# Attention with each head on one half of the array's rows, its scores and values sharing two PSUM banks, and v of each batch in its own buffers

## Chip, cores and metric

The kernel runs on one core of one Trainium2 chip. The metric is the device time of one execution in microseconds (us). Three runs of the kernel before gave 643.86, 646.71 and 646.88 us; the median, 646.71 us, is the time before.

## What is computed

The attention of 2 batches and 8 heads over 576 positions with 64 features per head, then two feed-forward layers on the 1152 tokens. Heads 0 to 3 see the last 32 positions, heads 4 to 7 see every fourth of the last 128 positions, so each query has 32 keys.

```
scores = scale * (q @ k.T)
rel = pos[:, None] - pos[None, :]
mask_plain = (rel >= 0) & (rel < 32)                      # heads 0..3
mask_dil = (rel >= 0) & (rel < 128) & (rel % 4 == 0)      # heads 4..7
attn = softmax(where(mask, scores, -1e9))
x = attn @ v                                              # [2, 8, 576, 64] -> [1152, 512]
h = x @ w_in;  x = (h * tanh(softplus(h))) @ w_out        # 512 -> 2048 -> 512
p = probs / (probs.sum(-1) + 1e-9)
out = sum_e p[:, e] * (relu(x @ w1[e]) @ w2[e])           # 4 experts, 512 -> 1024 -> 512
```

## The kernel before

**Units.** The attention is cut into 10 units: 2 batches by 5 chunks of 128 positions (the last chunk of a batch has 64). I number them 0 to 9. A unit holds all 8 heads of its chunk, as 4 pairs of heads; the two heads of a pair lie on partitions 0 to 63 and 64 to 127 of the transposed q and k. Pairs 0 and 1 are the plain heads, pairs 2 and 3 the dilated ones, whose positions are sorted by their remainder modulo 4, so that every block of 32 queries needs a run of 64 keys.

**One unit's work.** `load_qk` brings k and q in natural layout. `transposes` (L309) turns them on TensorE. `spread` (L318 to L324) copies them on ScalarE from PSUM to `kk` and `qq`. In `kk` the copy is spread: head 0 of a pair goes to columns j=0 on partitions 0 to 63, head 1 to columns j=1 on partitions 64 to 127, and the other halves are zero (`zero_k`, L210, on VectorE). A score matmul (L338, L343) has a block of 32 queries of both heads as its stationary operand (128 rows, 32 columns) and 128 columns of `kk` as its moving operand: 64 keys of one head and 64 of the other, with the zeros keeping the heads apart. The four query blocks write four strips of 32 partitions. Ahead of them `sel` and `msk` put the mask into the same PSUM bank (L330 to L333). `softmax` reads the maximum (L351) and subtracts it (L352) on VectorE and takes the exponential on ScalarE (L353); `sums` (L357 to L359) follows on VectorE. `probsT` (L365) transposes the probabilities, `probsT_copy` (L370, ScalarE) brings them to `pT`, `values` (L377, L381) multiplies 128-row blocks of `pT` by `vP` or `vD`, again with zeros beside each head's v (`zero_v`, L202 and L203, on GpSimd), `normalise` (L389, VectorE) divides, `xT` (L398) transposes back, and `x_hi` (L406, ScalarE) and `x_lo` (L410, VectorE) split x into a high and a low part for the layers.

**Banks.** Scores are in bank 2 (unit 1: bank 6), transposed probabilities in bank 3, values in bank 4, `xT` in bank 5, the transposes of k and q in banks 0 and 1 (unit 1: 4 and 5). Every bank is a tile of its own, 512 columns of float32.

**Order.** The order is written out by hand: each engine works through its instructions as the program issues them. `att_step(s)` issues, in this order: the copy of unit s-1's probabilities, the copies of v for unit s+1, `spread` of unit s+1, `scores` and `softmax` of unit s, `sums` and `values` of unit s-1, `xT` of unit s-2, `normalise` of s-1, `x_hi` and `x_lo` of s-2 (from s=5 on with a weight-decoding step between, `dec_dve` and `dec_act`), `transposes` of s+2, `probsT` of s, and then the loads. Unit 1's scores are issued in step 0 already. The last three units (`u3`, `u2`, `u1` are units 7, 8 and 9) are written out after the loop, mixed with the first matmuls of the first layer (`steps[0].first`, `steps[1].first` in two halves, `steps[0].second`).

**v.** v of a head pair lies in `vP` (plain) and `vD` (dilated): on partitions 32 to 63 (and 96 to 127) the block's own 32 keys, on 0 to 31 (and 64 to 95) the block before, which `copy_v` (L277, L279) copies on GpSimd. Both batches use the same buffer. `v_loads` says in which step which chunks are loaded; all loads go through the queue of SP in program order.

**Weights.** `dec_load` brings a packed half of w_in or w_out into one of four staging buffers (L132, L135), `dec_dve` (L151, L158) and `dec_act` (L168, L175, L176) unpack it. The first layer accumulates its output for the first 512 tokens in banks 0 to 3 (`steps[n].second`, L509) after L487.

Of the kernel before, what the change touches and what calls it, by code (L numbers as in the profile page):

```python
# [23 lines left out]
def kernel(  # L24
# [41 lines left out]

    def bank(n):
        return ps.tile([128, 512], F32, tag=f"bank{n}", name=nm("bank"))
# [130 lines left out]
    def zero_v(c):  # L199
        blk = slice(4 * c, min(4 * c + 4, S // 32))  # L200
        for j in range(2):
            POOL.memset(vP[64 * j:64 * j + 64, :, blk, 1 - j, :], 0.0)  # L202
            POOL.memset(vD[64 * j:64 * j + 64, :, 1 - j, c], 0.0)  # L203
            if c == 0:
                POOL.memset(vP[64 * j:64 * j + 32, :, 0, j, :], 0.0)
                POOL.memset(vD[64 * j:64 * j + 32, :, j, 0], 0.0)

    def zero_k(c):
        for j in range(2):
            DVE.memset(kk[64 * j:64 * j + 64, :, 1 - j, 128 * c + 128:128 * c + 256], 0.0)  # L210
# [7 lines left out]
    for lo in (0, 32):  # L218
        m = msk[lo:lo + 32, :]
# [6 lines left out]
    for j in range(2):  # L226
        DVE.memset(kk[:, :, j, 0:128], 0.0)
        DVE.memset(kk[:, 2:4, j, 128 * NCH:], 0.0)
    for j in range(2):
        DVE.memset(vD[64 * j + 32:64 * j + 64, :, j, NCH - 1], 0.0)  # L230
# [5 lines left out]
    zero_v(1)  # L236
    for g in range(4):
        for n in "ns" if g else "n":
            ACT.activation(sel[n][0:32, 32 * g:32 * g + 32], ident[0:32, 0:32], AF.Copy)
        for n in "f" if g else "sf":  # L240
            ACT.activation(sel[n][32:64, 32 * g:32 * g + 32], ident[32:64, 32:64], AF.Copy)

    t = bank(7)
# [3 lines left out]
    def msk_b(n):  # L247
        return msk.unsqueeze(1).to_broadcast([64, n, 64])

    def load_v(b, c0, c1):
# [3 lines left out]
        for j in range(2):  # L256
            own = slice(64 * j + 32, 64 * j + 64)
            for p in range(2):
                src = v[b, 2 * p + j:2 * p + j + 1]
                SP.dma_start(out=vP[own, p, g0:g1, j, :],  # L260
                             in_=bass.AP(src.tensor, src.offset + 32 * g0 * D, [[D, 32], [32 * D, g1 - g0], [1, D]]))
            src = v[b, 4 + j:5 + j]
            for p in range(2 if cf > c0 else 0):
                SP.dma_start(out=vD[own, p, j, c0:cf, :],
                             in_=bass.AP(src.tensor, src.offset + (2 * p * S + 128 * c0) * D,
                                         [[4 * D, 32], [128 * D, cf - c0], [1, 4 * D]]))
            if cf < c1:
                n = (S - 128 * cf) // 4
                SP.dma_start(out=vD[64 * j + 32:64 * j + 32 + n, :, j, cf, :],
                             in_=bass.AP(src.tensor, src.offset + 128 * cf * D, [[4 * D, n], [2 * S * D, 2], [1, 4 * D]]))  # L270

    def copy_v(c):

        g0, g1 = max(4 * c, 1), min(4 * c + 4, S // 32)
        for j in range(2):
            before, own = slice(64 * j, 64 * j + 32), slice(64 * j + 32, 64 * j + 64)
            POOL.tensor_copy(vP[before, :, g0:g1, j, :], vP[own, :, g0 - 1:g1 - 1, j, :])  # L277
            if c:
                POOL.tensor_copy(vD[before, :, j, c, :], vD[own, :, j, c - 1, :])  # L279


    v_loads = {-2: (0, 2, NCH), 2: (1, 0, 2), 4: (1, 2, 4), 5: (1, 4, NCH)}

    class Unit:
        def __init__(self, b, c):
# [5 lines left out]
            self.tbanks, self.sbank, self.s = ((4, 5), 6, None) if second else ((0, 1), 2, None)  # L291
# [20 lines left out]
        def spread(self):  # L312
            n, t0 = self.n, 128 * self.c
            for j in range(2):
                rows = slice(64 * j, 64 * j + 64)
                o = slice(128 + t0, 256 + t0)
                if n == 128:
                    ACT.activation(kk[rows, :, j, o], self.pt[0][rows], AF.Copy)  # L318
                else:
                    ACT.activation(kk[rows, 0:2, j, 128 + t0:128 + t0 + n], self.pt[0][rows, 0:2, 0:n], AF.Copy)  # L320
                    dst, src = (x.rearrange("p a (r i) -> p a r i", r=4)[:, :, :, 0:n // 4]
                                for x in (kk[rows, 2:4, j, o], self.pt[0][rows, 2:4]))
                    ACT.activation(dst, src, AF.Copy)
            ACT.activation(qq[:, :, t0:t0 + n], self.pt[1][:, :, 0:n], AF.Copy)  # L324

        def scores(self):
            n, c = self.n, self.c
            self.s = s = bank(self.sbank)
            if self.first:
                PE.matmul(s[:, 0:256], sel["s"], msk_b(4), start=True, stop=False, skip_group_check=True)  # L330
                PE.matmul(s[:, 256:512], sel["f"], msk_b(4), start=False, stop=False, skip_group_check=True)
            else:
                PE.matmul(s, sel["n"], msk_b(8), start=True, stop=False, skip_group_check=True)  # L333
# [6 lines left out]
            kr = kk.rearrange("p a j (c r i) -> p a j c r i", r=4, i=32)  # L340
            for p in range(2):
                for r in range(4):
                    PE.matmul(s[32 * r:32 * r + n // 4, 256 + 128 * p:384 + 128 * p],  # L343
# [598 lines left out]
```

## Time and profile before

| | |
|---|---|
| runs, median (lowest to highest) | 646.71 us (643.86 to 646.88) |
| profiled execution | 646.41 us |
| its span in the profile | 644.6 us |
| TensorE busy, share of the span | 98% |
| VectorE, ScalarE, GpSimd busy | 46%, 41%, 27% |
| granted TensorE clock, mean | 0.997 of full speed |

The profiled execution's own time is 1.8 us longer than the span that the profile shows, and 0.3 us below the median of the three runs. Times within the profile are in microseconds from the start of the span. Matmuls are pipelined: a line of the timeline gives the first start of a group and the time to the end of its last one, so a group's length holds the time for which one matmul passes through the array; how fast matmuls follow each other is read from the starts.

### The profile page before, as it was taken

How to read it: one execution, taken by the hardware profiler on the slowest of the kernel's cores; microseconds unless marked ns; L12 is line 12 of the kernel's file. 1: busy time of each engine (PE TensorE's matmuls, PEld its weight loads, DVE VectorE, ACT ScalarE, POOL GpSimd, SP SyncE). 2: the span in 40 equal slices, each digit the busy share in tenths (PEclk: the TensorE clock that was granted, in tenths of full speed). 3: DMA queues.
4: the chain of work that ended last, by engine and by line, in shares of the span. 5: the costliest groups of instructions: out<-in, count | busy, mean ns of one | idle time of the engine just before them, and what ended most of it. 6: DMA issues, size and time to landing. Idle time of an engine off the chain costs nothing.

```text
span 644.6 us, 10166 instructions
## 1 busy us (share of the span) xinstructions
PE 630.8 (98%) x4154; PEld 562.7 (87%) x4154; DVE 299.0 (46%) x488; ACT 261.5 (41%) x497; POOL 177.0 (27%) x195
## 2 busy tenths in 40 slices
PE   8988999999999999999999999999999999999997
PEld 5766888889999999989998899898899998899986
DVE  7778777622211325464543622534623444624223
ACT  6667877633232344443344322344322443322220
POOL 6736555521200143270134300143300234200000
PEclk9989999999999999999999999999999999999999
DMA  9976576400000222210023200033100022000102
GB/s 182 193 161 174 195 224 221 142 1 1 1 1 1 65 66 66 66 67 2 0 75 92 94 2 1 1 99 98 67 1 0 31 76 91 1 2 15 51 1 81
DMA packets 51358, 43.66 MB, mean 68 GB/s; under 512 B 26352, under 2 KB 44144, under 8 KB 51312
## 3 DMA queue, kind: packets, MB, share of 16 engines
q1 hardware_dynamic: 51312, 43.02, 23.8%
q8 instruction: 32, 0.52, 0.3%
q14 instruction: 14, 0.11, 0.1%
HBM read 40.65 MB, written 2.36 MB: 67 GB/s over the span
## 4 chain that ended last, share of the span: by engine, by line
PE 93%; DMA 3%; DVE 1%; SPq 1%; issue 1%; ACT 1%; POOL 0%; DVEq 0%; ACTq 0%; POOLq 0%
PE bank L745 31%; PE bank L692 28%; PE bank L509 16%; PE bank L487 15%; DMA natq<-in_q_dram 2%; PE bank L309 1%; SPq L298 1%; DMA scr<-in_moe_w_out_dram 1%; PE bank L398 1%; PE bank L377 0%; PE bank L365 0%; DVE scr L158 0%; PE bank L381 0%; DMA vD<-in_v_dram 0%; PE bank L338 0%
## 5 line engine op out<-in xcount | busy, mean ns | idle before, releaser
L692 PE MATMUL bank<-xh,late 128*128 128x256 f32 (+1 forms) x512 | 120.6, 297 | 0.6 <-ACT late L704 0.5
L692 PE MATMUL bank<-wxh,late 128*128 128x320 f32 (+1 forms) x384 | 94.7, 296 | 0.0
L692 PEld LDWEIGHTS bank<-xh,late 128*128 128x128 f32 x512 | 88.3, 188 | 4.9 <-ACT late L704 2.0
L745 PE MATMUL bank<-late,gh 128*128 128x512 f32 x288 | 89.3, 391 | 0.0
L487 PE MATMUL bank<-xh,late 128*128 128x320 f32 (+1 forms) x288 | 76.5, 337 | 0.0
L692 PE MATMUL bank<-xl,late 128*128 128x256 f32 (+1 forms) x256 | 75.3, 294 | 0.0
L648 POOL TENSOR_TENSOR raw<-raw 128x256 f32<-128x256 f32 x16 | 12.2, 764 | 221.7 <-DVE late L537 217.7
L509 PE MATMUL bank<-gh,late 128*128 128x320 f32 (+1 forms) x288 | 72.6, 337 | 0.0
L692 PEld LDWEIGHTS bank<-wxh,late 128*128 128x128 f32 x384 | 67.8, 188 | 0.0
L496 DVE TENSOR_TENSOR gl<-scr,gh 128x512 fp32r<-128x512 f32 (+1 forms) x32 | 24.6, 769 | 84.5 <-ACT gh L495 84.5
L745 PEld LDWEIGHTS bank<-late,gh 128*128 128x128 f32 x288 | 52.3, 188 | 9.7
L710 DVE TENSOR_TENSOR raw<-bank,late 128x256 f32<-128x256 f32 (+1 forms) x32 | 14.6, 457 | 98.4 <-PE bank L692 91.2
L492 ACT ACTIVATE scr<-bank 128x320 f32<-128x320 f32 (+1 forms) x48 | 23.5, 490 | 85.7 <-PE bank L487 85.7
L537 POOL TENSOR_TENSOR late<-raw,late 128x1024 fp32r<-128x1024 f32 x16 | 38.6, 2413 | 66.4 <-ACT late L536 66.4
L745 PE MATMUL bank<-late,gl 128*128 128x512 f32 x144 | 56.7, 394 | 0.0
L692 PE MATMUL bank<-wxl,late 128*128 128x256 f32 (+1 forms) x192 | 56.3, 293 | 0.0
L536 ACT ACTIVATE late<-raw 128x512 fp32r<-128x512 f32 (+1 forms) x64 | 48.3, 783 | 18.3 <-PE bank L745 16.7
L487 PEld LDWEIGHTS bank<-xh,late 128*128 128x128 f32 x288 | 50.7, 188 | 4.3
L509 PEld LDWEIGHTS bank<-gh,late 128*128 128x128 f32 x288 | 50.1, 188 | 4.3
L745 PE MATMUL bank<-late,late 128*128 128x512 f32 (+1 forms) x219 | 52.8, 388 | 0.0
L692 PEld LDWEIGHTS bank<-xl,late 128*128 128x128 f32 x256 | 48.1, 188 | 2.5
L487 PE MATMUL bank<-xl,late 128*128 128x320 f32 (+1 forms) x144 | 48.6, 337 | 0.0
(146 smaller groups left out, 1175.0 us busy)
## 6 DMA issues: line engine op xcount, KB each, us to landing
raw<-in_moe_w_dram SPq DMA_DIRECT2D x32, 512.0 KB, 3.6
raw<-in_moe_w_in_dram SPq DMA_DIRECT2D x16, 512.0 KB, 4.4
raw<-in_moe_w_out_dram SPq DMA_DIRECT2D x8, 512.0 KB, 4.0
scr<-in_moe_w_out_dram SPq DMA_DIRECT2D x8, 512.0 KB, 3.8
natk<-in_k_dram SPq DMA_DIRECT2D x8, 256.0 KB, 4.7
natq<-in_q_dram SPq DMA_DIRECT2D x8, 256.0 KB, 5.1
out_dram<-scr SPq DMA_DIRECT2D x8, 256.0 KB, 2.0
vD<-in_v_dram SPq DMA_DIRECT2D x16, 64.0 KB, 3.6
```

The costliest lines, as they stand in the source:

```text
L298: SP.dma_start(out=t[0:self.n], in_=(k if x == "k" else q)[self.b, :, rows, :].rearrange("h t d -> t h d"))
L309: PE.transpose(o, nat[0:n, 128 * a:128 * a + 128], ident[0:n, 0:n])
L487: PE.matmul(h, a[:, c, :], x[:, c, :], start=c == 0 and k == 0, stop=c == 3 and k == 2)
L492: ACT.activation(self.hc[:, self.w * i:self.w * (i + 1)], h, AF.Mish)
L496: DVE.tensor_tensor(out=self.glo, in0=self.hc, in1=self.ghi.bitcast(F32), op=ALU.subtract)
L509: PE.matmul(yacc[self.grp][d], a[:, 512 + 128 * d:640 + 128 * d], x[:, g], start=u == UORD[self.grp][0] and k == 0, stop=u == UORD[self.gr ...
L536: ACT.activation(hi, src, AF.Copy)
L537: eng.tensor_tensor(out=lo, in0=src, in1=hi.bitcast(F32), op=ALU.subtract)
L648: POOL.tensor_tensor(out=a22, in0=a21, in1=a22, op=ALU.add)
L692: PE.matmul(out, w, x(k), start=first and k == 0 and i == 0, stop=k == 1 and i == 2, skip_group_check=not first)
L710: DVE.tensor_tensor(out=self.cb[:, 0:N], in0=self.c, in1=p1, op=ALU.add)
L745: PE.matmul(acc, x[:, s], a[:, cols], start=self.p == 0 and f == 0 and i == 0, stop=self.p == NP2 - 1 and f == 1 and i == 2, skip_group_ch ...
```

## The change

All eight banks become slices of one tile. `kk` loses its doubled layout and its zeros: one head of a pair is on partitions 0 to 63, the other on 64 to 127, and each matmul takes one head, 64 rows, as operands. Every score and value matmul is thus two, one on either half of the rows, with 64 moving columns in place of 128. The two halves write two banks: scores of head j go to bank 2+j, columns 0 to 255 (unit 1: banks 6 and 7), values of head j to bank 2+j, columns 256 to 511. Transposed probabilities move from bank 3 to bank 4, unit 1's transposes to banks 5 and 6. The mask is put in by two matmuls of 256 columns in place of one of 512. `spread` copies k in one instruction per unit (two for a chunk of 64) instead of two (four). `vP` and `vD` get a buffer for each batch and lose their zeros, and batch 1's v is loaded one step earlier. In the closing part `u1.normalise` is issued before `steps[0].second`.

```diff
+    banks = ps.tile([128, 4096], F32, name="banks")
     def bank(n):
-        return ps.tile([128, 512], F32, tag=f"bank{n}", name=nm("bank"))
+        return banks[:, 512 * n:512 * (n + 1)]
...
-    kk = ap1.tile([128, 4, 2, 128 * (NCH + 1)], F32, name="kk")
+    kk = ap1.tile([128, 4, 128 * (NCH + 1)], F32, name="kk")
-    vP = ap1.tile([128, 2, S // 32, 2, D], F32, name="vP")
-    vD = ap1.tile([128, 2, 2, NCH, 4 * D], F32, name="vD")
+    vP = [ap1.tile([128, 2, S // 32, D], F32, name=f"vP{b}") for b in range(B)]
+    vD = [ap1.tile([128, 2, NCH, 4 * D], F32, name=f"vD{b}") for b in range(B)]
-    msk = ap1.tile([64, 64], BF16, name="msk")
-    sel = {n: ap1.tile([64, 128], BF16, name=f"sel{n}") for n in "nsf"}
+    msk = ap1.tile([128, 64], BF16, name="msk")
+    sel = {n: ap1.tile([128, 128], BF16, name=f"sel{n}") for n in "nsf"}
+    HEAD = [slice(64 * j, 64 * j + 64) for j in range(2)]
...
-    for c in range(NCH):
-        zero_k(c)
-    zero_v(0)
+    for b in range(B):
+        for j in range(2):
+            DVE.memset(vD[b][64 * j + 32:64 * j + 64, :, NCH - 1], 0.0)
+            POOL.memset(vP[b][64 * j:64 * j + 32, :, 0, :], 0.0)
+            POOL.memset(vD[b][64 * j:64 * j + 32, :, 0], 0.0)
...
-    v_loads = {-2: (0, 2, NCH), 2: (1, 0, 2), 4: (1, 2, 4), 5: (1, 4, NCH)}
+    v_loads = {-2: (0, 2, NCH), 1: (1, 0, 2), 3: (1, 2, 4), 4: (1, 4, NCH)}
...
-            self.tbanks, self.sbank, self.s = ((4, 5), 6, None) if second else ((0, 1), 2, None)
+            self.tbanks, self.sbank, self.s = ((5, 6), 6, None) if second else ((0, 1), 2, None)
...
-            for j in range(2):
-                rows = slice(64 * j, 64 * j + 64)
-                if n == 128:
-                    ACT.activation(kk[rows, :, j, o], self.pt[0][rows], AF.Copy)
+            if n == 128:
+                ACT.activation(kk[:, :, o], self.pt[0], AF.Copy)
...
-            self.s = s = bank(self.sbank)
+            self.s = banks[:, 512 * self.sbank:512 * self.sbank + 1024].rearrange("p (j x) -> p j x", j=2)[:, :, 0:256]
+            s = [self.s[:, j] for j in range(2)]
...
-                    PE.matmul(s[32 * g:32 * g + 32, 128 * p:128 * p + 128], qq[:, p, t:t + 32],
-                              kk[:, p, :, t + 96:t + 160], start=False, stop=True, skip_group_check=True)
+                    for j, h in enumerate(HEAD):
+                        PE.matmul(s[j][32 * g:32 * g + 32, 64 * p:64 * p + 64], qq[h, p, t:t + 32],
+                                  kk[h, p, t + 96:t + 160], start=False, stop=True, skip_group_check=True)
...
         def probsT(self):
-            pt = bank(3).rearrange("p (s t) -> p s t", s=4)
+            pt = bank(4).rearrange("p (s t) -> p s t", s=4)
...
         def values(self):
-            self.x = x = bank(4).rearrange("p (s d) -> p s d", s=4)
+            self.x = banks[:, 1024:2048].rearrange("p (j x) -> p j x", j=2)[:, :, 256:512].rearrange(
+                "p j (s d) -> p j s d", d=D)
-                    PE.matmul(x[32 * g:32 * g + 32, p, :], self.pT[:, p, 32 * g:32 * g + 32],
-                              vP[:, p, 4 * c + g].rearrange("p j d -> p (j d)"), start=True, stop=True)
+                    for j, h in enumerate(HEAD):
+                        PE.matmul(self.x[32 * g:32 * g + 32, j, p], self.pT[h, p, 32 * g:32 * g + 32],
+                                  vP[b][h, p, 4 * c + g], start=True, stop=True, skip_group_check=True)
...
-        if 0 <= s < NCH - 2:
-            zero_v(s + 2)
...
     steps[0].split()
     dec_act()
+    u1.normalise()
     steps[0].second(lo_last=True)
-    u1.normalise()
```

## Rows read from the trace of the kernel before

**Rows 1.** The page's chain that ended last, shares of the span by engine.
```profile
PE 93%; DMA 3%; DVE 1%; SPq 1%; issue 1%; ACT 1%; POOL 0%; DVEq 0%; ACTq 0%; POOLq 0%
```

**Rows 2.** Busy time by stretch: stretch, length, each engine's busy us (instructions), granted clock, DMA.
```profile
100.00:110.00 10.00, 10.00 (x45) 8.05 (x44) 7.77 (x11) 7.39 (x13) 6.25 (x5) 1.00 0.67 213
```

**Rows 3.** TensorE timeline, unit 5's step: start, length, what, count, [idle before <-releaser].
```profile
30.58 0.28 PE L330 MATMUL bank<-msk,sels 64*128 64x256 bf16 x1
...
30.89 0.65 PE L338 MATMUL bank<-kk,qq 128*32 128x128 f32 x16
...
31.79 0.50 PE L377 MATMUL bank<-vP,pT 128*32 128x128 f32 x6
...
32.77 0.65 PE L398 MATMUL bank<-ident,xn 128*128 128x128 f32 x4
...
34.18 0.66 PE L365 MATMUL bank<-ident,pr 128*128 128x128 f32 x4
34.77 0.39 PE L333 MATMUL bank<-msk,seln 64*128 64x512 bf16 x1
```

**Rows 4.** VectorE timeline of the same step: maximum and subtraction of unit 5.
```profile
32.04 0.69 DVE L351 TENSOR_REDUCE mx<-bank 128x8 f32<-128x512 f32 x1 [0.35 <-PE bank L343]
32.77 0.69 DVE L352 TENSOR_TENSOR pr<-bank,mx 128x512 f32<-128x512 f32 x1
```

**Rows 5.** TensorE timeline: matmuls of 64 moving columns, and two on different strips.
```profile
20.57 0.41 PE L309 MATMUL bank<-ident,natq 64*128 64x64 f32 x4
...
27.05 0.28 PE L338 MATMUL bank<-kk,qq 128*32 128x128 f32 x2
```

**Rows 6.** Groups by line to 66 us: count, busy us, mean ns, idle before and releaser.
```profile
L210 DVE MEMSET kk<- 64x512 f32 x10 | 4.8, 485 | 1.5 <-issue 0.5
...
L318 ACT ACTIVATE kk<-bank 64x512 f32<-64x512 f32 x16 | 9.4, 587 | 1.3 <-PE bank L309 1.2
```

**Rows 7.** Chain that ended last, in order of time: two loads of q.
```profile
5.37 5.17 DMA natq<-in_q_dram
...
19.95 5.30 DMA natq<-in_q_dram
```

**Rows 8.** TensorE timeline: the values of units 5 and 6, with the idle time before.
```profile
37.58 0.64 PE L377 MATMUL bank<-vP,pT 128*32 128x128 f32 x16 [1.42 <-ACT pT L370]
...
43.67 1.02 PE L377 MATMUL bank<-vP,pT 128*32 128x128 f32 x16 [1.73 <-issue]
```

**Rows 9.** Busy time by stretch as in rows 2, around the values of unit 6.
```profile
40.36:43.77 3.41, 1.68 (x40) 1.04 (x42) 2.36 (x5) 1.94 (x4) 0.00 (x0) 1.00 1.15 218
43.77:47.18 3.41, 3.41 (x42) 2.70 (x42) 1.81 (x5) 2.54 (x5) 1.25 (x3) 0.50 0.57 99
```

**Rows 10.** Chain that ended last, in order of time, into the first layer.
```profile
50.25 3.89 DMA scr<-in_moe_w_out_dram
...
54.24 0.44 DVE scr L151
...
59.13 0.70 DVE pr L352
59.86 0.64 ACT pr L353
...
60.54 0.67 PE bank L365 x4
...
64.52 3.01 PE bank L509 x12
```

**Rows 11.** TensorE timeline: values of unit 8 and the transposes behind them.
```profile
56.94 0.64 PE L377 MATMUL bank<-vP,pT 128*32 128x128 f32 x16 [0.53 <-POOL vD L279]
...
57.95 0.66 PE L398 MATMUL bank<-ident,xn 128*128 128x128 f32 x4
```

**Rows 12.** VectorE timeline: normalise of unit 9, in two pieces.
```profile
65.11 0.74 DVE L389 TENSOR_TENSOR xn<-bank,sm 64x256 f32<-64x256 f32 x2
```

**Rows 13.** SP's queue: loads of batch 1's last chunk of v, then the weights.
```profile
45.74 2.59 SPq L260 DMA_DIRECT2D vP<-in_v_dram  x2
```

More of the change, by code (lines that the diff above doesn't have):

```diff
@@ L217 @@
     POOL.memset(msk, 0.0)
-    for lo in (0, 32):
-        m = msk[lo:lo + 32, :]
+    for o in range(0, 128, 32):
+        m, lo = msk[o:o + 32, :], o % 64
         POOL.affine_select(out=m, in_=m, compare_op=ALU.is_ge, fill=NEG, base=32,
@@ L225 @@
         DVE.memset(t, 0.0)
[L226 to L230, printed above, removed]
-    for c in range(NCH):
-        zero_k(c)
-    zero_v(0)
+    DVE.memset(kk[:, :, 0:128], 0.0)
+    DVE.memset(kk[:, 2:4, 128 * NCH:], 0.0)
+    for b in range(B):
[3 more added lines that the diff above has]
+            POOL.memset(vD[b][64 * j:64 * j + 32, :, 0], 0.0)
     for t in free_raws:
         POOL.memset(t[:, 4096:4104].bitcast(U32), 0)
[L236 to L241, printed above, removed]
+    for o in range(0, 128, 32):
+        eye = ident[o:o + 32, o:o + 32].unsqueeze(1)
+        for n, g0, g1 in (("n", 0, 4), ("s", 1, 4)) if o % 64 == 0 else (("f", 0, 4), ("s", 0, 1)):
+            dst = sel[n][o:o + 32, 32 * g0:32 * g1].rearrange("p (g i) -> p g i", i=32)
+            ACT.activation(dst, eye.to_broadcast([32, g1 - g0, 32]), AF.Copy)
     t = bank(7)
@@ L245, with msk_b @@
         PE.matmul(t, warm[:, 0:128], warm, start=n == 0, stop=n == NWARM - 1)
[L247 to L248 removed]
+    def msk_b(j, n):
+        return msk[HEAD[j]].unsqueeze(1).to_broadcast([64, n, 64])
     def load_v(b, c0, c1):
@@ L259, in load_v @@
                 src = v[b, 2 * p + j:2 * p + j + 1]
-                SP.dma_start(out=vP[own, p, g0:g1, j, :],
+                SP.dma_start(out=vP[b][own, p, g0:g1, :],
                              in_=bass.AP(src.tensor, src.offset + 32 * g0 * D, [[D, 32], [32 * D, g1 - g0], [1, D]]))
@@ L263, in load_v @@
             for p in range(2 if cf > c0 else 0):
-                SP.dma_start(out=vD[own, p, j, c0:cf, :],
+                SP.dma_start(out=vD[b][own, p, c0:cf, :],
                              in_=bass.AP(src.tensor, src.offset + (2 * p * S + 128 * c0) * D,
@@ L268, in load_v, with copy_v @@
                 n = (S - 128 * cf) // 4
-                SP.dma_start(out=vD[64 * j + 32:64 * j + 32 + n, :, j, cf, :],
+                SP.dma_start(out=vD[b][64 * j + 32:64 * j + 32 + n, :, cf, :],
                              in_=bass.AP(src.tensor, src.offset + 128 * cf * D, [[4 * D, n], [2 * S * D, 2], [1, 4 * D]]))
-    def copy_v(c):
+    def copy_v(b, c):
         g0, g1 = max(4 * c, 1), min(4 * c + 4, S // 32)
@@ L276, in copy_v @@
             before, own = slice(64 * j, 64 * j + 32), slice(64 * j + 32, 64 * j + 64)
-            POOL.tensor_copy(vP[before, :, g0:g1, j, :], vP[own, :, g0 - 1:g1 - 1, j, :])
+            POOL.tensor_copy(vP[b][before, :, g0:g1, :], vP[b][own, :, g0 - 1:g1 - 1, :])
             if c:
-                POOL.tensor_copy(vD[before, :, j, c, :], vD[own, :, j, c - 1, :])
-    v_loads = {-2: (0, 2, NCH), 2: (1, 0, 2), 4: (1, 2, 4), 5: (1, 4, NCH)}
+                POOL.tensor_copy(vD[b][before, :, c, :], vD[b][own, :, c - 1, :])
+    v_loads = {-2: (0, 2, NCH), 1: (1, 0, 2), 3: (1, 2, 4), 4: (1, 4, NCH)}
     class Unit:
@@ L313, in spread @@
             n, t0 = self.n, 128 * self.c
-            for j in range(2):
-                rows = slice(64 * j, 64 * j + 64)
-                o = slice(128 + t0, 256 + t0)
-                if n == 128:
-                    ACT.activation(kk[rows, :, j, o], self.pt[0][rows], AF.Copy)
[L319 to L323, printed above, removed]
+            o = slice(128 + t0, 256 + t0)
+            if n == 128:
+                ACT.activation(kk[:, :, o], self.pt[0], AF.Copy)
+            else:
+                ACT.activation(kk[:, 0:2, 128 + t0:128 + t0 + n], self.pt[0][:, 0:2, 0:n], AF.Copy)
+                dst, src = (x.rearrange("p a (r i) -> p a r i", r=4)[:, :, :, 0:n // 4]
+                            for x in (kk[:, 2:4, o], self.pt[0][:, 2:4]))
+                ACT.activation(dst, src, AF.Copy)
             ACT.activation(qq[:, :, t0:t0 + n], self.pt[1][:, :, 0:n], AF.Copy)
@@ L327, in scores @@
             n, c = self.n, self.c
-            self.s = s = bank(self.sbank)
[L329 to L333, printed above, removed]
+            self.s = banks[:, 512 * self.sbank:512 * self.sbank + 1024].rearrange("p (j x) -> p j x", j=2)[:, :, 0:256]
+            s = [self.s[:, j] for j in range(2)]
+            for k in range(2) if self.first else (0,):
+                for j, h in enumerate(HEAD):
+                    if self.first:
+                        PE.matmul(s[j][:, 128 * k:128 * k + 128], sel["sf"[k]][h], msk_b(j, 2), start=k == 0, stop=False,
+                                  skip_group_check=True)
+                    else:
+                        PE.matmul(s[j], sel["n"][h], msk_b(j, 4), start=True, stop=False, skip_group_check=True)
             t0 = 128 * c
@@ L792 @@
     u3.probsT_copy()
-    copy_v(u1.c)
+    copy_v(u1.b, u1.c)
     u1.spread()
```

45 lines of the change are left out of this document (20 added, 25 removed).

## The prediction

> **What bounds the kernel now.** I read four views in this order. First the page's chain that ended last: 93% of it is TensorE [rows 1], so the kernel is a queue of matmuls. Then the busy time by stretch: from about 65 us on, a stretch like 100 to 110 us has TensorE busy for all of its 10.00 us at the full granted clock [rows 2]. The change touches nothing there, so whatever it gains or loses is the shift of the first layer's start, one for one. Third the TensorE timeline of the attention, 0 to 65 us. A full step in its middle lasts 34.77 - 30.58 = 4.19 us with no idle bracket: mask, scores, values of the unit before, xT, two transposes, probsT [rows 3]. VectorE takes its 1.42 us for maximum and subtraction (32.04 to 32.77 + 0.69) beside the values and transposes [rows 4]. So the middle is bound by TensorE. Elsewhere it isn't: early on by loads of q and k, one of which lands at 10.54 us and one at 25.25 [rows 7], and late by the decoding of weights, which holds up the copy of the probabilities (waits of 1.42 and 1.73 us before the values of units 5 and 6 [rows 8]). Last the chain in order of time: the first layer's second matmuls start at 64.52, and what leads there is no attention matmul. It is a load of weights landing at 50.25 + 3.89 = 54.14, VectorE from 54.24 to the end of unit 9's subtraction at 59.82, the exponential, probsT at 60.54, and ScalarE's work up to 64.52 [rows 10].
>
> **What the change does, part by part.**
>
> *Matmuls.* Scores and values take eight rounds of four matmuls each now: the four strips run side by side (two matmuls on different strips take 0.28 us together, about the 0.27 of one [rows 5]), and the 32 matmuls of a unit's scores take 31.79 - 30.89 = 0.90 us, 0.11 a round [rows 3]. Afterwards there are 64 matmuls of 64 columns. What 64 columns cost shows in the half chunk's transposes: four in 0.41, less the 0.22 that one takes to pass, is 0.063 each [rows 5]. No row shows two matmuls on different halves of the rows. Either they overlap like the strips (8 x 0.063 = 0.50) or they go in turn (1.00). I take 0.50, since column strips are the nearest row and do overlap: -0.38 for scores, -0.38 for values. The mask as two matmuls of 256 columns, one on either half, saves 0.11 if they overlap and nothing if not.
>
> By the Trainium skill (TensorE: Matmul & The Clock Gate, "Wait — 56ns, not 53.3ns?") starts never come closer than about 25 ns. The two matmuls in 0.28 us disagree: they start at most 0.01 us apart [rows 5]. By the page, 64 matmuls would take 1.60 us in place of 0.50; rival 3 is near this.
>
> *The new wait.* Scores stood in bank 2 and values in bank 4. Now both stand in banks 2 and 3, at different columns. In each step the program issues scores of unit s, softmax of s, values of s-1. The kernel writes no waits itself. I take it that the layer under it orders any two engines that use one bank, so values of s-1 must wait until VectorE has subtracted the maximum from the scores of s. The Trainium skill (PSUM — Partial Sum Buffer, "PSUM bank collisions raise a hardware error") says that two engines may not touch one bank in the same partitions at once, whatever the columns; no run here shows it. Behind the waiting values stand, on TensorE, xT of s-2, the transposes of s+2 and probsT of s, and behind probsT all of the next step. A full step is then one chain: mask to scores 0.31 - 0.11 = 0.20; scores to maximum 32.04 - 30.89 = 1.15, less 0.38, 0.77; maximum and subtraction 1.42; the signal 0.05 (the subtraction's end at 59.82 to ScalarE's start at 59.86 is 0.04 [rows 10]); values to xT 32.77 - 31.79 = 0.98, less 0.38, 0.60; xT to probsT 1.41; probsT to mask 0.59 [rows 3, 4]. Sum 5.04, against 4.19: each such step gets 0.85 us longer although TensorE has 0.87 less to do.
>
> *Where these 0.85 us go.* Up to unit 2 I expect nothing to move, since loads of q and k pace the start [rows 7]. From unit 2 to unit 6 the steps are TensorE's: four times 0.85 is +3.4 if all of it counts, less where the q that lands at 25.25 stays the bound; I take +2.3. At units 5 and 6 the values wait 1.42 and 1.73 us today for ScalarE's copy [rows 8]. The new wait runs in the same time, so there the shorter matmuls count, about -0.8 each. And after the longer of these waits the granted clock stood at 0.50 from 43.77 to 47.18 [rows 9], up to half of 3.41 us lost; at the new pace I expect that stretch to end no later than today. So at unit 8 I take the delay as zero, give or take 1.5.
>
> *The tail.* Here the wait decides. Values of unit 8 start at 56.94 today, xT of unit 7 1.01 later at 57.95 [rows 11]. They will wait for unit 9's subtraction, which ends at 59.82 because VectorE decodes until then [rows 10]. So: 59.87 + 0.63 for the values, 0.44 + 0.05 for xT, six matmuls of the first layer at 0.23 (3.01 us for twelve, less the pass of the last [rows 10]) 1.38: probsT of unit 9 at 62.37 in place of 60.54, +1.83. From there to the second matmuls the same 3.98 us. Their third accumulator is bank 2, where unit 9's values lie: after four matmuls (0.92) they wait for normalise, which ends at 65.11 + 0.74 = 65.85 today [rows 12], 1.33 after the second matmuls' start, since on VectorE it stands behind the split. That adds 0.46 with the signal. Sum +2.3.
>
> *v.* Batch 1's v no longer waits for batch 0's, and its loads move up a step on SP's queue, past the loads of q and k of units 7 and 9 and two loads of weights. q of unit 7 comes some 4 us later and is still in time, since its transposes move later too. The queue's last six loads of v (two took 2.59 us [rows 13]) then no longer stand right ahead of the load that lands at 54.14. It could land up to 3.6 us sooner; VectorE can use about 1.4 of this, because before it comes unit 7's normalise, itself behind unit 8's subtraction. Bounds: 0 to -1.4; I take the middle, -0.7.
>
> *Zeros and copies.* Ten VectorE memsets of 0.49 us fall away and 0.59 us of ScalarE per unit [rows 6]; the first softmax comes earlier, and the load of q waits all the same [rows 7]. GpSimd's zeroing lay beside its waits for loads. Cost and gain 0; if that cover went, a step would gain at most 0.6.
>
> *Sum.* 2.3 - 0.7 = +1.6. The profiled execution took 646.41 us (span 644.6, 1.8 outside it), 0.3 below the median of the three runs: 646.4 + 1.6 = **648.0 us**. A measurement of this kernel can tell about 0.5%, 3.2 us, from no change.
>
> **Rivals.**
> 1. *The clock drops again and again.* After the idle 1.42 us the clock stayed at 2.4 GHz, after 1.73 it was 1.2 GHz for 3.41 us [rows 8, 9]. TensorE had been busy for 1.68 us between 40.36 and 43.77. The new idle time is about 1.6 a step (0.05 + 1.42 and the pass of the scores), between the two, eight times over. For it: the closeness to 1.73. Against it: the 1.42. TensorE streams about 2.9 of 5.04 us, so a stretch of 3.41 at half speed costs some 1.1 net; four of them 4.4, of which the tail's decoding covers 1.6: +1.6 + 2.8, **650.8 us**. It decides for slower from three stretches on.
> 2. *The halves go in turn.* Then each step costs 1.1 more (0.50, 0.50, 0.11), eight steps 8.8, of which the waits of rows 8 cover 3.2: +1.6 + 5.6, **653.6 us**. The change would not do what it says.
> 3. *Every matmul has its turn, whatever its columns.* The 32 that take 0.90 us, 0.028 each [rows 3], become 64 that take 1.80: 1.3 more than 0.50 for scores and for values, eight steps 20.8, less 3.2: +1.6 + 17.6, **665.6 us**. The two starts within 0.01 us speak against it [rows 5].
> 4. *No wait between softmax and values*, because they use different columns. Then the middle steps gain 0.8, and the tail's chain stays, up to 1.4 sooner by the earlier load: **645.0 us**. For it: different bytes; against: one bank.
>
> **How the numbers follow.** Forecast 0.54 (0.02 faster, 0.47 same, 0.05 slower by over 0.5%), clock 0.23 (0.03 same, 0.20 slower), halves in turn 0.06 slower, every matmul in its turn 0.02 slower, no wait 0.15 (0.06 faster, 0.09 same). Faster 0.08, same 0.59, slower 0.33. The range goes from 644.5 (no wait, most of it) to 653.6 (halves in turn), which leaves out about 2 in 10. The forecast's own range, by the bounds of the load and the give or take at unit 8, is 645.8 to 650.2.
>
> **What would show it.** TensorE's idle bracket before the values (L377's successor) of units 2 to 6, 1.4 to 1.6 us, released by VectorE's subtraction; mask to mask about 5.0 us there; 16 + 16 score matmuls per half with starts 0.063 us a round; unit 8's values after unit 9's subtraction; the second matmuls at 64.8 to 66.3 and an idle bracket within them. The prediction is wrong if values start before the subtraction ends, if a block of scores takes about 1.0, if the granted clock is 0.50 in several stretches between 17 and 60 us, or if TensorE has new gaps behind 70 us.

## The result, and the profile after

The changed kernel takes 655.9 us (median of six runs, 652.2 to 658.8) against 646.8 before: 1.015 of the time, interval 1.011 to 1.019. It is slower by 9.1 us, where 648.0 was forecast and the range ended at 653.6.

First the busy time by stretch, from the mask of unit 2 to the mask of unit 9 in each kernel (columns as in [rows 2]; the last three rows are experiments of the next section):

| kernel | stretch, us | length | TensorE busy (matmuls) | granted clock |
|---|---|---|---|---|
| before | 16.97 to 55.03 | 38.06 | 33.15 (558) | 0.96 |
| after | 17.47 to 67.37 | 49.90 | 35.56 (998) | 0.79 |
| e3, the wait alone | 18.57 to 61.98 | 43.41 | 31.89 (563) | 1.00 |
| e6, the halves alone | 18.14 to 61.28 | 43.14 | 34.28 (997) | 0.82 |
| e8, after with dummy matmuls | 17.68 to 64.86 | 47.18 | 37.05 (1027) | 0.96 |

The span grew by 12.4 us in the profiled execution (657.0 for 644.6; it is the slowest of the six), and 11.8 of it lie in this stretch. The tail behind it took 9.17 us up to the first layer's second matmuls (67.37 to 76.54 in the timeline), 0.32 less than before (55.03 to 64.52 [rows 10]):

```profile
76.54 0.50 PE L501 MATMUL banks<-gh,wxh 128*128 128x512 f32 x1 [0.66 <-ACT gh L487]
...
77.92 0.51 PE L501 MATMUL banks<-gh,wxh 128*128 128x512 f32 x1 [0.19 <-DVE xn L383]
```

How late the units are shows in their masks: unit 8 before (unit 6 began at 34.77 [rows 3]), then units 6 and 8 after.

```profile
48.02 0.39 PE L333 MATMUL bank<-msk,seln 64*128 64x512 bf16 x1
```

```profile
47.53 0.40 PE L320 MATMUL banks<-msk,seln 64*128 64x256 bf16 x2
...
60.02 0.28 PE L320 MATMUL banks<-msk,seln 64*128 64x256 bf16 x2
```

Second, TensorE's timeline after, as in [rows 3]: unit 2's step and the values of unit 1; unit 4's mask, the values of unit 3, unit 5's mask; and the scores of unit 5. L317 and L320 are the mask, L326 and L332 the scores, L369 the values.

```profile
17.69 0.46 PE L326 MATMUL banks<-kk,qq 64*32 64x64 f32 x32
17.95 0.59 PE L332 MATMUL banks<-kk,qq 64*32 64x64 f32 x32
20.15 0.45 PE L369 MATMUL banks<-vP,pT 64*32 64x64 f32 x31 [1.60 <-DVE pr L341]
...
32.12 0.28 PE L320 MATMUL banks<-msk,seln 64*128 64x256 bf16 x2
...
34.70 0.45 PE L369 MATMUL banks<-vP,pT 64*32 64x64 f32 x31 [1.61 <-DVE pr L341]
...
35.48 0.66 PE L392 MATMUL banks<-ident,xn 128*128 128x128 f32 x4
...
37.38 0.23 PE L317 MATMUL banks<-msk,sels 64*128 64x128 bf16 x2
...
37.86 0.51 PE L332 MATMUL banks<-kk,qq 64*32 64x64 f32 x22
40.92 0.33 PE L332 MATMUL banks<-kk,qq 64*32 64x64 f32 x10 [2.55 <-issue]
```

Three things stand there. The halves overlap: the first 32 of a unit's 64 score matmuls start within 17.95 - 17.69 = 0.26 us, where before 16 larger ones took 0.43 to 0.47 for the same work (0.90 for the unit [rows 3]). The values wait 1.6 us for the subtraction L341 in each step (twice, for 1.71 and 1.60 us, the profile names a load of v and GpSimd as what came last); a step at full clock with this wait takes 37.38 - 32.12 = 5.26 us, for 4.19 before. And in the middle of a block of scores TensorE stands still for 2.55 us with nothing named that it waits for.

Third, the stretches in which the clock was low (columns as in [rows 2]):

```profile
20.90:31.10 10.20, 8.28 (x183) 6.70 (x183) 4.40 (x9) 3.04 (x7) 6.92 (x13) 0.50 0.79 161
...
41.40:48.20 6.80, 5.32 (x94) 4.62 (x99) 4.35 (x9) 2.52 (x5) 2.33 (x4) 0.50 0.56 144
51.70:55.10 3.40, 3.40 (x32) 2.85 (x38) 1.96 (x4) 1.99 (x4) 0.51 (x1) 0.50 0.15 40
```

That is 20.4 us at 1.2 GHz in three stretches, six times the 3.41 us of before [rows 9]. The waits of TensorE, summed (line, releaser: us in total, times, longest), and the queue of instructions from the page's part on DMA queues:

```profile
PE banks L369 <- DVE pr L341: 9.7, 6, 1.6
PE banks L332 <- issue: 2.5, 1, 2.5
```

```profile
q8 instruction: 37, 0.61, 0.4%
```

The same line of before says 32 and 0.52 MB: TensorE's 4,774 matmuls, for 4,154, come with five more loads of instructions of 16 KB each.

### The profile page after: what moved, and what is told of

Same layout as the page of the kernel before. It is cut to its first block, busy times and chain, and to the rows that moved or that the text cites. A ratio compares the mean times of both kernels' runs of the same rounds, so it can differ in the third digit from the quotient of the medians.

```text
span 657.0 us, 11321 instructions
## 1 busy us (share of the span) xinstructions
PE 630.8 (96%) x4774; PEld 564.3 (86%) x4774; DVE 291.4 (44%) x478; ACT 255.0 (39%) x481; POOL 169.7 (26%) x183
## 4 chain that ended last, share of the span: by engine, by line
PE 93%; SPq 2%; DVE 2%; issue 1%; DMA 1%; ACT 1%; POOL 0%; DVEq 0%; POOLq 0%; ACTq 0%
PE banks L737 30%; PE banks L684 27%; PE banks L501 15%; PE banks L479 15%; PE banks L392 1%; SPq L284 1%; PE banks L295 1%; SPq L246 1%; PE banks L369 1%; DMA natq<-in_q_dram 1%; DVE mx L340 1%; DVE pr L341 1%; PE banks L355 1%; PE banks L374 1%; PE banks L332 0%
## 5 line engine op out<-in xcount | busy, mean ns | idle before, releaser
L684 PE MATMUL banks<-xh,late 128*128 128x256 f32 (+1 forms) x512 | 120.7, 297 | 0.6 <-ACT late L696 0.5
L684 PE MATMUL banks<-wxh,late 128*128 128x320 f32 (+1 forms) x384 | 94.6, 296 | 0.0
L684 PEld LDWEIGHTS banks<-xh,late 128*128 128x128 f32 x512 | 88.3, 188 | 4.9 <-ACT late L696 2.0
L737 PE MATMUL banks<-late,gh 128*128 128x512 f32 x288 | 89.3, 391 | 0.0
L479 PE MATMUL banks<-xh,late 128*128 128x320 f32 (+1 forms) x288 | 76.5, 337 | 0.0
L684 PE MATMUL banks<-xl,late 128*128 128x256 f32 (+1 forms) x256 | 75.3, 294 | 0.0
L501 PE MATMUL banks<-gh,late 128*128 128x320 f32 (+1 forms) x288 | 72.6, 337 | 0.0
L684 PEld LDWEIGHTS banks<-wxh,late 128*128 128x128 f32 x384 | 67.8, 188 | 0.0
L737 PE MATMUL banks<-late,gl 128*128 128x512 f32 x144 | 56.8, 394 | 0.0
L684 PE MATMUL banks<-wxl,late 128*128 128x256 f32 (+1 forms) x192 | 56.3, 293 | 0.0
L479 PEld LDWEIGHTS banks<-xh,late 128*128 128x128 f32 x288 | 50.7, 188 | 4.3
```

Of the source, the lines that this page charges most:

```text
L479: PE.matmul(h, a[:, c, :], x[:, c, :], start=c == 0 and k == 0, stop=c == 3 and k == 2)
L501: PE.matmul(yacc[self.grp][d], a[:, 512 + 128 * d:640 + 128 * d], x[:, g], start=u == UORD[self.grp][0] and k == 0, stop=u == UORD[self.gr ...
L684: PE.matmul(out, w, x(k), start=first and k == 0 and i == 0, stop=k == 1 and i == 2, skip_group_check=not first)
L737: PE.matmul(acc, x[:, s], a[:, cols], start=self.p == 0 and f == 0 and i == 0, stop=self.p == NP2 - 1 and f == 1 and i == 2, skip_group_ch ...
```

## The experiments

### What the wait costs, and what it hangs on

**e3_waitonly** puts scores and values of the kernel before into shared banks 2 and 3 and leaves its full-height matmuls as they are. As in the changed kernel, transposed probabilities go to bank 4 and unit 9's normalise is issued earlier. The edit of the values:

```
...
-            self.x = x = bank(4).rearrange("p (s d) -> p s d", s=4)
+            self.x = x = banks[:, 1024:2048].rearrange("p (k x) -> p k x", k=2)[:, :, 256:512].rearrange(
+                "p k (s d) -> p k s d", s=2)
...
```

> The kernel before, with its zeros and its matmuls of 128 rows, but scores of the plain heads in bank 2 and of the dilated heads in bank 3 (256 columns each) and values in the other halves of banks 2 and 3, so that values wait for the softmax as in the changed kernel. Only the wait is added, the matmuls keep their length. Summed from the rows of before: 0.31 + 1.15 + 1.42 + 0.05 + 0.98 + 1.41 + 0.59 = 5.91 us per step against 4.19. Theory A: TensorE streams longer per step, but idles the same 1.6 us; half-speed stretches as in the changed kernel, 655 to 660 us. If the shorter matmuls are what lets the clock fall, there are none or one, and the time is 651 to 654 us. Theory C: 646 to 648 us.

Measured: 653.5 us, 1.0105 (1.0073 to 1.0137), +7.6 us, at a clock of 1.000.

```profile
PE banks L380 <- DVE pr L353: 8.2, 5, 1.6
```

```profile
36.37 0.28 PE L333 MATMUL banks<-msk,sels 64*128 64x256 bf16 x1
...
42.30 0.39 PE L333 MATMUL banks<-msk,seln 64*128 64x256 bf16 x2
...
54.10 0.39 PE L333 MATMUL banks<-msk,seln 64*128 64x256 bf16 x2
```

Its steps take 42.30 - 36.37 = 5.93 us from mask to mask, 1.74 more than 4.19: the whole wait comes on top of the matmuls, step after step. So a loss of this size, most of the changed kernel's 9.1, can come without any halves and without a low clock.

**e11_split_reads** cuts the maximum and the subtraction of the changed kernel in two, one for each bank.

```
-            DVE.tensor_reduce(out=mx, in_=sv, axis=AX.X, op=ALU.max)
+            for j in range(2):
+                DVE.tensor_reduce(out=mx[:, j], in_=sv[:, j], axis=AX.X, op=ALU.max)
...
```

> The changed kernel with its maximum and its subtraction cut in two each, one instruction for each bank, so that no read spans from bank 2 into bank 3; scores and values still share banks 2 and 3. Theory V (the wait of 1.6 us belongs to the view that spans both banks: the e10 kernel waited 1.63 us although its values had a bank that its scores did not use, but that lay between theirs): the values' waits for the subtraction fall below 0.5 us each, and the time comes to what e1 and e6 have, 649 to 652 us, with issue stalls in its place. Rival S (the wait belongs to the bank that both write, whatever the reads are): the waits stay at 1.6 us or grow by the two added instructions, 655 to 659 us.

```profile
PE banks L372 <- DVE pr L344: 8.8, 7, 1.3
```

The wait stays; it is 1.3 for 1.6 because the subtraction of bank 2 now ends before that of bank 3. 656.9 us, 1.0149 (1.0120 to 1.0179). So sharing the bank is enough; the view over two of them isn't needed for it. **e7_apart_fill** shows the same by accident. It gives the values banks of their own (as e1, below) and sets dummy matmuls into columns 0 to 255 of bank 7, of which the values use 256 to 511:

```
+            for i in range(6):
+                PE.matmul(banks[:, 3584:3840], warm[:, 0:128], warm[:, 0:256], start=i == 0, stop=i == 5, skip_group_check=True)
```

> e1_apart with six dummy 256-column bf16 matmuls on zeros in steps 2 to 7, ahead of the transposes that wait for q and k, into an unused part of a bank. They cost 6 x 0.11 = 0.64 us a step where TensorE does not wait anyway. Theory C (e1's loss against the kernel before, 5.3 us, is its 10.2 us at half speed): granted clock 0.997 or more, no stretch at half speed before 80 us, and 646 to 648.5 us. Rival (the loss is waits for loads and instruction fetches, and the low clock only accompanies them): 651 us or more.

```profile
PE banks L446 <- DVE xn L384: 13.4, 6, 2.5
```

The dummies wait for the normalise of other columns of that bank, 2.2 us a step. So e7 failed at its own question (657.3 us at a clock of 0.997 say nothing of the clock) and answers this one. **e10_scores_halves** has its scores alone on halves, in banks 2 and 7, read as one view with a step of five banks, and its values in bank 4:

```
+                self.s = by2[:, slice(0, 3, 2) if u == 9 else slice(2, 8, 5), 0:256]
...
```

> The kernel before with the scores alone on row halves, in all units but the second (two banks that the values don't use, so nothing waits; values, loads and v buffers as before). Some 124 matmuls a step for 88, the scores about 0.40 us shorter. Theory F: as e9, 646.5 to 650 us with issue stalls at piece boundaries. Rival: 9 x 0.40 = 3.6 us less, 642.5 to 645 us.

```profile
PE banks L411 <- DVE pr L378: 7.0, 4, 2.0
```

Values in a bank that the scores never touch wait too, so the order is kept for the whole range that a view spans (e12 below, with neighbouring banks and the values outside them, has no such wait). 655.1 us, 1.0144 (1.0116 to 1.0171); with this wait it says nothing of the halves.

### The halves without the wait

**e1_apart** gives the values of the changed kernel banks 6 and 7 (the first and the last two units other pairs):

```
-            self.x = banks[:, 1024:2048].rearrange("p (j x) -> p j x", j=2)[:, :, 256:512].rearrange(
+            a = 512 * {0: 2, 8: 0, 9: 2}.get(5 * self.b + self.c, 6)
+            self.x = banks[:, a:a + 1024].rearrange("p (j x) -> p j x", j=2)[:, :, 256:512].rearrange(
...
```

> The changed kernel, but the values of units 1 to 7 go to banks 6 and 7 and those of unit 8 to banks 0 and 1, so that no bank holds scores and values at once. Theory A (the shared banks cause the wait, and the idle time of 1.6 us per step lets the clock fall to 1.2 GHz): no idle bracket before the values, granted clock 0.50 for at most one stretch of 3.4 us, and a time of about 645 us, the 645.0 that the prediction gave for no wait. Theory B (the wait alone costs, the clock only goes with it): the same 645 us, but half-speed stretches may stay. Theory C (the 1240 additional matmuls and weight loads cost by themselves, the wait does not matter): still above 652 us.

Measured: 651.1 us, 1.0079 (1.0052 to 1.0106). No wait for a subtraction is left, and still +5.3 us. In its place stand waits for q and k, and 10.2 us at 1.2 GHz from 48.8 on (mean clock 0.992):

```profile
PE banks L295 <- DMA natq<-in_q_dram: 5.5, 8, 1.6
PE banks L295 <- DMA natk<-in_k_dram: 2.6, 3, 1.3
```

What the shorter blocks are worth shows in its timeline too, in a step that waits for nothing: the scores of unit 2 go from 18.17 to the values at 18.86, 0.69 us for 0.90.

```profile
18.17 0.46 PE L326 MATMUL banks<-kk,qq 64*32 64x64 f32 x32
18.44 0.59 PE L332 MATMUL banks<-kk,qq 64*32 64x64 f32 x32
18.86 0.45 PE L370 MATMUL banks<-vP,pT 64*32 64x64 f32 x30
```

**e6_apart_vlate** puts batch 1's loads of v back to their old steps:

```
-    v_loads = {-2: (0, 2, NCH), 1: (1, 0, 2), 3: (1, 2, 4), 4: (1, 4, NCH)}
+    v_loads = {-2: (0, 2, NCH), 2: (1, 0, 2), 4: (1, 2, 4), 5: (1, 4, NCH)}
```

> e1_apart (row halves, values in banks of their own, no wait) with batch 1's v loads back at steps 2, 4 and 5. Theory L (e1's waits for q and k, 5.5 and 2.6 us, come from the v loads that now stand ahead of them in SP's queue): these waits fall below 5 us together, and the time to 646 to 649. Rival (the order of the loads does not matter; TensorE simply reaches its operands sooner with the shorter blocks, and the rest is clock): within 1.5 us of e1's 651.1.

The waits for q and k fell to 2.1 us, as the theory on the loads said, and the time stayed: 651.6 us, 1.0097 (1.0065 to 1.0128). What took their place (TensorE's timeline, the rows with an idle time put down to issue):

```profile
21.02 0.45 PE L375 MATMUL banks<-vD,pT 64*32 64x64 f32 x29 [1.01 <-issue]
...
26.15 0.35 PE L370 MATMUL banks<-vP,pT 64*32 64x64 f32 x17 [1.50 <-issue]
...
30.14 0.36 PE L370 MATMUL banks<-vP,pT 64*32 64x64 f32 x19 [0.24 <-issue]
...
34.35 0.33 PE L332 MATMUL banks<-kk,qq 64*32 64x64 f32 x10 [0.63 <-issue]
...
39.62 0.34 PE L332 MATMUL banks<-kk,qq 64*32 64x64 f32 x14 [1.19 <-issue]
...
45.26 0.21 PE L326 MATMUL banks<-kk,qq 64*32 64x64 f32 x1 [1.83 <-issue]
```

All six are in the middle of a block, where nothing is waited for. Counted from the first matmul of the trace, the one that comes late is number 348, 474, 600, 727, 853 and 979: one in 126. The changed kernel's two (21.11 and 40.92) are numbers 348 and 727, of the same row; the kernel before has one too, 0.35 us at 20.07. That is the size of one load of instructions (620 more matmuls, five more loads: 124 each); I call the matmuls of one load a piece. From 26.15 to 45.26 every piece came late, 19.1 us for four of them, 4.8 each. A step has 146 matmuls here (64 + 64, 16 transposes, 2 masks), for 81 before, so each step needs a new piece. The 4.8 us are not a fixed price: in e5 below two loads start 3.9 us apart (21.40 and 25.25) and the piece is in time.

The loads themselves stand in the traces. Of the changed kernel, from 38.0 to 38.5 us (packets, MB, share of 16 engines):

```profile
q8 instruction: 1, 0.02, 16.1%
```

This load starts at 38.14 and takes 1.29 us (0.161 of 16 engines' 0.5 us); TensorE goes on at 40.92, 1.49 us after its end. It is the same at all 27 idle times of this kind that the traces of this case show: the load of the late piece ended 1.2 to 1.8 us before its first matmul and started 2.2 to 3.2 us before it, when TensorE had already begun 17 to 125 of the 126 matmuls of the piece before. The load takes 0.9 to 1.6 us, no longer than later in the layers; it starts late, and dense blocks use up the rest of the old piece before it is there. What makes it start is not shown.

How much of the 5.3 us is late pieces (6.4 us in all here) and how much is the clock is not shown either: this run has 17.1 us at 1.2 GHz, from 16.3 and from 47.0 on, a mean of 0.986.

**e2_fill** shows from another side that the place is a number, not an instruction. It adds five dummy matmuls a step, into the wait of steps 2 to 7:

```
+            for i in range(5):
+                PE.matmul(t, warm[:, 0:128], warm, start=i == 0, stop=i == 4)
```

> The changed kernel with its wait, but five matmuls of 512 bf16 columns of zeros into bank 7 stand on TensorE between scores and values in steps 2 to 7 (5 x 0.21 us, about the length of the wait); in the tail the wait stays empty. Nothing else changes; the result of these matmuls is not used. Theory A: clock at 2.4 GHz through most of the attention, mask to mask still about 5.0 us, and 648 to 650 us, the sum of the prediction without its clock. Theory B: about as slow as the changed kernel, 655 us, since the wait is still there. Theory C: 655 us or more.

```profile
36.00 0.38 PE L332 MATMUL banks<-kk,qq 64*32 64x64 f32 x7
38.95 0.43 PE L332 MATMUL banks<-kk,qq 64*32 64x64 f32 x25 [2.58 <-issue]
```

Three steps, 15 dummies: the gap behind the 22nd matmul of L332 moved to behind the 7th. e2 has two more such idle times (2.18 and 2.07 us) and takes 660.5 us, 1.0218 (1.0190 to 1.0246); its clock was low for 3.4 us from 16.7 on, held then to 57.6 us and fell for 10.2.

**e5_count** leaves the kernel before as it is but cuts each product into two of 64 columns, so it has the changed kernel's instructions (4,762 matmuls, 37 loads) and none of its parts:

```
-                    PE.matmul(s[32 * g:32 * g + 32, 128 * p:128 * p + 128], qq[:, p, t:t + 32],
-                              kk[:, p, :, t + 96:t + 160], start=False, stop=True, skip_group_check=True)
+                    for j in range(2):
+                        a = 128 * p + 64 * j
+                        PE.matmul(s[32 * g:32 * g + 32, a:a + 64], qq[:, p, t:t + 32],
+                                  kk[:, p, j, t + 96:t + 160], start=False, stop=True, skip_group_check=True)
...
```

> The kernel before with every attention product cut into two 64-column matmuls (the full-height zero-padded operands stay, so do the banks and the loads): the number of TensorE instructions of the changed kernel (4,774 matmuls for 4,154) without its halves, its shared banks or its early v loads. Theory F (the instruction stream of TensorE is brought in pieces of 16 KB, 37 for 32 in the changed kernel, and a denser stream runs out of it): 36 or 37 instruction fetches, one or more idle times of 1 to 3 us put down to issue in the middle of a block of matmuls, and 648 to 651 us. Rival (the number of instructions costs only what the blocks themselves show): blocks of 32 taking at most 0.9 us for 0.46, no such idle times, 646 to 649 us with every loss inside the blocks.

648.6 us, 1.0049 (1.0031 to 1.0067). Its blocks are no longer than before (32 in 0.48 us). Two idle times lie at piece ends, 0.41 and 1.02 us (numbers 346 and 722). The third, 1.55 at number 1003, isn't one: there the values of unit 6 wait for ScalarE's copy, as in [rows 8]. So the number alone costs 2.3 us, of which the piece ends show 1.4; the others of its pieces, at 145 matmuls a step of 4.3 us and more, are in time.

### One half of the halves

**e9_values_halves** and **e12_scores_halves2** are the kernel before with the values alone, or the scores alone, on halves, all in banks of their own (units 0 to 7, or all but unit 1); e13 is e9 with unit 7's values in another pair of banks.

```
+                        PE.matmul(self.x[32 * g:32 * g + 32, j, p], self.pT[h, p, 32 * g:32 * g + 32],
+                                  vP[h, p, 4 * c + g, j], start=True, stop=True, skip_group_check=True)
...
```

> The kernel before with the values alone on row halves, in units 0 to 7 (two banks of their own, so nothing waits; scores, loads and v buffers as before). A step then has some 120 matmuls for 88, and its values take about 0.40 us less. Theory F (TensorE's instructions come in pieces of some 128 matmuls, and e6 and e5 got one piece per 4.0 to 5.8 us in the attention): 120 matmuls a step cannot come faster than about 4.2 to 4.5 us, so nothing is gained: issue stalls at several piece boundaries, 646.5 to 650 us. Rival (without the shared banks the shorter blocks pay): 8 x 0.40 = 3 us less, 643 to 645 us.

> The e10 kernel (scores alone on row halves) with its scores in neighbouring banks 2 and 3 and its values in bank 7, so that no view spans a bank of the values. No waits of 1.6 us. Theory F (instructions come at one piece of 128 matmuls per 4.0 to 5.8 us; some 124 matmuls a step): issue stalls of 2 us or more in all, and 646 to 650 us. Rival (the scores are part of the chain from mask to transposed probabilities, so 0.40 us a step come off the end): 9 x 0.40 = 3.6 us less, 642.5 to 645 us.

> The e9 kernel (values alone on row halves) with unit 7's values in banks 0 and 1, which takes away a wait of 2.2 us of the first layer for a bank. If that wait was on the path, 646.95 - 2.2 + up to 0.5 for the wait for the copies from banks 0 and 1 = 644.7 to 645.3 us, 0.998 to 0.999 of the kernel before; if an instruction stall or a softmax chain takes its place, 646 to 647.

e9 took 646.95 us, 1.0026 (1.0011 to 1.0041); e12 647.5, 1.0015 (1.0002 to 1.0029); e13 647.1, 1.0018 (1.0006 to 1.0029). A step has 113 or 114 matmuls (not the 120 and 124 that the expectations count). There is no wait of values for a subtraction, at most one late piece in each (none in e9, 1.89 us in e12, 0.84 in e13), and no gain. So several late pieces, as theory F has them, are not what takes the gain. e9 has a wait of 2.19 us of the first layer for unit 7's normalise in a bank; e13 hasn't, and is no faster. e9's steps are still 4.19 us long (22.28 to 26.47), since there the chain from scores over softmax to probsT doesn't get shorter. Two rows of its timeline:

```profile
25.19 0.63 ACT L357 ACTIVATE pr<-pr 128x512 f32<-128x512 f32 x1 [0.98 <-DVE pr L356]
...
25.88 0.66 PE L369 MATMUL banks<-ident,pr 128*128 128x128 f32 x4
```

The exponential ends at 25.82, and the transposes of the probabilities start at 25.88. e12's steps without a wait are shorter (21.41 - 17.47 = 3.94), and against what it gains stand its late piece (1.89) and the values of unit 6, which wait 2.41 us for ScalarE's copy, where before waited 1.73 [rows 8]. None of the versions beats the kernel before.

### The clock, and the loads of v

**e8_fill_all** is e2 with dummies in the waits of all steps from 2 to 9:

> The changed kernel with five dummy 512-column matmuls on zeros in the wait of every step from 2 to 9 (e2_fill had them to step 7, and its clock fell in the tail for 10.2 us). Theory C (the clock is what the changed kernel loses beyond its wait): no half-speed stretch between 20 and 80 us, and 648 to 653 us. Rival F (at full clock the instruction stream runs out instead, as e2_fill's three idle times of 2.1 to 2.6 us say): idle times put down to issue of 4 us or more in all, and 655 us or more although the clock is up.

Its clock is 0.997 (3.4 us at half speed are left), the steps without a late piece take 5.26 us (17.68 to 22.94), so the dummies lie in the wait and cost nothing there, and the time is 656.2 us, 1.0153 (1.0131 to 1.0174): no gain. Five late pieces stand in its timeline, three of them here:

```profile
43.56 0.24 PE L326 MATMUL banks<-kk,qq 64*32 64x64 f32 x1 [2.57 <-issue]
...
49.78 0.39 PE L326 MATMUL banks<-kk,qq 64*32 64x64 f32 x22 [0.81 <-issue]
...
54.83 0.66 PE L392 MATMUL banks<-ident,xn 128*128 128x128 f32 x4 [1.79 <-issue]
```

With 0.71 and 0.86 before them they are 6.7 us, for 3.0 in the changed kernel. That fits a picture in which half-speed stretches leave the instructions time to come; it is not tested by itself. But among the changed kernel's own six runs the time does go with the clock: 652.2 us at 0.994, 658.8 at 0.984, 6.7 us for 6.6 us of clock lost (0.006 x 650.4 and 0.016 x 657.0). So what the clock costs by itself stays open; that a full clock, reached with dummies, doesn't bring the loss back is shown.

**e4_vlate** is the changed kernel with the loads of v at their old steps (e6's diff).

> The changed kernel with batch 1's v loaded in steps 2, 4 and 5 as before, still into its own buffer. The prediction gave the earlier loads 0 to 1.4 us: then 656 to 657.5 us. If they take the place of loads of q and of weights that are waited for, it is under 655 us.

659.2 us, 1.0206 (1.0157 to 1.0256), at a clock of 0.974 in the profile: outside both ranges, not faster than the changed kernel, and its clock is too low to say more. With e1 beside e6 (1.0079 and 1.0097) the early loads are worth nothing that these runs can tell from zero.

## Why the prediction was wrong, step by step

- *Matmuls: the mechanism right, the gain half of the forecast.* Halves overlap like strips, but a unit's scores take 0.69 us where 0.50 was forecast (e1), and its values up to xT 0.78 (34.70 to 35.48 after) where 0.60 was: 0.2 gained each, not 0.38. The second 32 matmuls of a block, the dilated ones, take longer than the first (0.42 for 0.27 in e1). The Trainium skill's floor of about 25 ns between starts (TensorE: Matmul & The Clock Gate, "Wait — 56ns, not 53.3ns?") does not hold on separate parts of the array: 32 starts in 0.26 us are 8 ns apart. So rivals 2 and 3 fall.
- *The new wait: right.* Released by the subtraction, as forecast; a step of 5.26 us for 5.04, since the blocks are longer than forecast. That one bank is enough, whatever the columns, was assumed, and e7 and e11 show it. Rival 4 falls.
- *Where the delay goes: wrong, and this is the step that failed.* Forecast were +2.3 us at unit 6 and none at unit 8. The changed kernel's unit 6 is 12.8 us late (47.53 for 34.77) and its unit 8 still 12.0 (60.02 for 48.02). "At unit 8 I take the delay as zero" was an offset by the waits of [rows 8] and the lost clock of [rows 9]; it took back 0.8. In e3, where only the wait is added, it took back 1.5: unit 6 is 7.5 us late (42.30 for 34.77), unit 8 6.1 (54.10 for 48.02), and unit 2 was 1.6 late already. The steps from unit 2 to unit 6 take 30.06 us after (17.47 to 47.53) for 17.80 before. Four steps of 5.26 and the two late pieces make 24.0 of them; some 6 are left for a stretch with 16.3 us at 1.2 GHz, an estimate from these rows and not a test.
- *The tail: wrong the other way.* +2.3 was forecast because unit 9's subtraction stood behind the decoding of weights. With the middle this late, the subtraction follows its scores at once, and the tail is 0.3 shorter than before.
- *The clock rival: half-speed stretches came, but its reason for them is not enough.* It was to decide from three stretches of 3.41 us on; there are six of them, 20.4 us, and the prediction had named them as a sign of being wrong. It put them down to an idle time between 1.42 and 1.73 us in each step. e3 has idle times of 1.58 to 1.70 in eight steps, and its clock is 1.000. So the idle time alone doesn't lower the clock; what does is open. Its price, 650.8 us, was too low as well. The reason given against it, that 1.42 us of idle time had not lowered the clock, was one row for a case that repeats in every step.
- *Not in the prediction at all: the supply of instructions.* The change was costed by the time of its matmuls; that there are 620 more was only looked at as starts. e6 shows pieces of 126 matmuls coming late six times in a row, and e5 that the number costs 2.3 us by itself. The halves, whose shorter blocks gain some 0.4 us a step once the wait is gone, lose 5.3 in all, with the clock's part in it.
- *v: not settled* (-0.7 forecast; e1 and e6 differ by 0.0018 of the time, less than either interval). *The second matmuls* do wait for unit 9's normalise within, 0.19 us for 0.46.

The wait alone costs 7.6 us (e3), the halves alone 5.3 (e1, e6), both together 9.1: less than the sum. Instructions that come during the wait would explain that; it was not tested. What stays open is the clock's own share, and what makes a load of instructions start as late as it does.

## To carry to other kernels

Before work is cut into more and smaller matmuls, count them: divide a step's matmuls by what one load of instructions holds, and ask whether dense blocks use up a piece in less than the 2.2 to 3.2 us that passed here from the start of a load to its first matmul. Look at which engine still reads a bank when something else is put into its free columns, since the order is kept for the bank. And when a delay is said to be swallowed later, name the wait that swallows it and test it with the wait alone.

## What the runs showed of the hardware

- TensorE's instructions are a stream that can run dry. They come in loads of 16 KB, one for about 126 matmuls with their weights. A load takes 0.9 to 1.6 us, and the late pieces began 2.2 to 3.2 us after its start. The Trainium skill (Runtime: NRT & Kernel Launch, "Instruction fetch mechanics") says 256 instructions to a block of 16 KiB, the next one fetched while the current one runs, which agrees with 126 pairs; that crossing a block is "mostly hidden" does not hold in these attention steps (0.24 to 2.58 us each in the kernels with more matmuls).
- 32 matmuls of 64 rows and 64 columns on eight parts of the array start in 0.26 us, 8 ns apart. The layer under the kernel keeps the order between engines for a bank, also where the columns differ (e7, e11), and for the banks that a view steps over (e10).
- The same wait of 1.6 us in every step went with a clock of 1.2 GHz for 20.4 us in the changed kernel (steps of 5.26 us and more) and with no fall at all in e3 (1.000, steps of 5.9 us, longer matmuls). Before the changed kernel's first fall, at 20.9 us, TensorE had stood idle from 18.55 to 20.15.
